# Linear attention into a gated feed-forward layer: weight pieces and block sums in one transfer each, and a new table of ranks

## The chip, the core and the metric

One core of one Trainium2 chip runs the whole kernel. The metric is device time in microseconds (us), the median of several executions. Trace times count from the start of the span, the first instruction of the program.

## What is computed

```python
def phi(x):
    proj = einsum('bhsd,df->bhsf', x, w_phi)
    proj = proj - max(abs(proj), axis=-1, keepdims=True)
    return concatenate([exp(proj), exp(-proj)], axis=-1)
q_p, k_p = phi(q), phi(k)
kv = einsum('bhsf,bhsd->bhfd', k_p, v); z = sum(k_p, axis=2)
num = einsum('bhsf,bhfd->bhsd', q_p, kv)
den = einsum('bhsf,bhf->bhs', q_p, z)[..., None] + 1e-06
x = (num / den) as 4608 tokens x 512            # 8 batches x 576, 8 heads x 64
g = x @ w_gate
out = (silu(g) * (x @ w_val)) @ w_out           # 512 -> 1536 -> 512
```

The three weight matrices are float64, q, k, v and w_phi float32.

## The kernel before

**Attention** works on pairs of heads, 32 pairs in all (8 batches of 4). For a pair it loads k, v and q, projects them on TensorE, takes the largest magnitude on VectorE, the exponentials on ScalarE, and ends with a division and a transposition that write x in two parts, xh (rounded) and xl (the rest). The first eight pairs make the first three chunks of 384 tokens.

**The feed-forward layer** multiplies every number as a rounded part plus a rest, with three matmuls per product (high x high, high x low, low x high), and turns the float64 weights into such parts with a chain on VectorE and ScalarE (weight_piece, lines 382 to 441: lines 403 to 419 are the VectorE steps). The twelve tiles f of the hidden width are converted one after the other while the first three chunks pass, and stored in DRAM: w1_dram for the first layer, w2_dram and w2_whole for the second. The gate of a chunk is lines 896 to 901.

**From chunk 4 on** two chunks at a time are done with seven block products instead of eight, in both layers. For the first layer the operands are seven "units" of weights per f. load_unit (line 1070) loads a pair of units into a slot of the buffers w1 (the trace says w) or of the space a2 (the trace says a); line 1081 is that load, 512 KB for two units. For the second layer the weights are needed as seven "pieces" of 128 x 1536: three are quarters of w_out as it is (BLOCKS 0, 2 and 3), four are sums of such quarters. sums_of_units (line 1234) makes the sums: for each q of six it loads the four quarters of two f into a stage of the buffer spare (line 1238), GpSimd forms the differences (line 1241), line 1246 stores them to w2_sums. piece_of_weights (line 1252) loads one piece (line 1257 for a sum, line 1261 for a quarter), then three copies on ScalarE (line 1267) and three subtractions on VectorE (line 1268) split it. Pieces 0 to 2 are made as soon as the sums are stored, long before the second layer's products (line 1396) begin; pieces 3 to 6 later.

**The order of work** comes from a planner that runs when the program is built. Every instruction, or small group, is a Step with an engine, a cost, the steps it follows and a rank. Plan.run plays the steps through with these costs, takes on each engine the ready step of the lowest rank, and among equal ranks the one added first, and writes the instructions in that order; on the chip each engine then works through its list in order, SyncE's DMA issues among them. Attention pair i has rank i, the feed-forward's short steps FIRST = -1, loads of units and everything of pieces NEXT = -0.5, its matmuls 1000 and up. A DMA is a step of SyncE that takes 0.6 or 0.34 us of it, and the wire for its bytes over BYTES. A load of units must also follow the product that lies 10 us before its use in planned time (ahead(AHEAD[2])):

```python
held[g] = k, first_, add("SP", n * P * 4 * P * 4, lambda: nc.sync.dma_start(...),
    [stored_, *after, ahead(AHEAD[2])], NEXT)
```

The table MOVED gives single steps another rank, by the number of the step in the order of adding. Its keys reach to about 1480 of 5291 steps. Numbers 0 to 455 or so are the attention of the first eight pairs, those up to 1370 the conversion of weights and the first three chunks, the rest up to 1480 belong to pair 8.

Of the kernel before, what the change touches and what calls it, by code (L numbers as in the profile page):

```python
# [59 lines left out]


MOVED = {
# [9 lines left out]


class Step:
# [8 lines left out]
class Plan:  # L83
# [1 line left out]


    LAG = {"PE": 220, "ACT": 90, "DVE": 90, "POOL": 200, "SP": 2000}
    BYTES = 340.0
    BEGIN = {"PE": 1000.0}

    def __init__(self, banks, extra, first):
# [26 lines left out]
    def run(self):  # L118
# [11 lines left out]
        def start(e):  # L130
            nonlocal n, wire, other
            held = []
            got, saved = None, False
            while ready[e]:
                key, s = heapq.heappop(ready[e])
                if s.take is not None and (saved or len(s.take) > sum(len(x) for x in self.lists(s))):
                    held.append((key, s))
                    saved = True
                    continue
                got = s  # L140
                break
            for h in held:
                heapq.heappush(ready[e], h)
            if got is None:
                if e == "PE" and self.fill is not None and pending():
                    cost, fn = self.fill
                    fn()
                    busy[e] = True
                    n += 1
                    heapq.heappush(events, (now + cost, n, "free", e))  # L150
                return
            s = got
            for t in s.take or ():
                self.bank[t] = next(x for x in self.lists(s) if x).pop(0)
            s.fn()
            busy[e] = True
            cost = s.cost
            if e == "PE":
                cost += TURNED if s.rank >= 1000 and other else 0
                other = s.rank < 1000  # L160
            if e == "SP":
                wire = max(wire, now) + s.cost / self.BYTES
                freed, done = now + (600.0 if s.cost < 1e5 else 340.0), wire + s.lag
            else:
                freed, done = now + cost, now + cost + s.lag
            n += 1
            heapq.heappush(events, (freed, n, "free", e))

            for t in s.then:
                n += 1  # L170
                heapq.heappush(events, (freed if t.eng == e and e in ("ACT", "DVE", "PE", "POOL") else done, n, "dep", t))
            if s.give is not None:
                n += 1
                heapq.heappush(events, (done, n, "give", s.give))
# [26 lines left out]

LANDING = {"x": 3000.0, "h": 3000.0, "w": 2500.0, "f": 0.0}
FILL = 200
STRIPS = 350
MERGED = 200
TURNED = 0
KEXP = (1, 0)
BIASED = (0,)  # L210
QEXP = 0
SWITCH = 125
POOLED = 950
INPUT = 1.36
SLOW = 2.0
NEXT_KEYS = 0


# [14 lines left out]


def pe(n):
    return max(58, 7 + 0.441 * n)


def pe32(n):
# [4 lines left out]
def favor_attention_moe(ctx: ExitStack, tc: tile.TileContext, qT, kT, v, w_phi, wg, wv, wo, out):  # L244
# [213 lines left out]
    def keys_of(i, rank):  # L458
# [10 lines left out]
        if i == EARLY_PAIRS + 1:  # L469
            def clear():  # L470
                nc.gpsimd.memset(vf[1]()[:, :, :, D:], 1.0)
                for h in range(2):
# [2 lines left out]
            last["vf", i - 2] = last["kin", i - 2] = last["qin", i - 2] = add("POOL", 1000, clear, weights_done, rank)  # L475
        before = lambda name: [last.get((name, i - 2)), last.get((name + "'", i - 2))]

        k_in = [add("SP", INPUT * P * 4 * P * 4, lambda: nc.sync.dma_start(get(kin[one])[:, :4 * P], kT[b, pr, :, :4 * P]),
                    before("kin"), rank)]
        k_in += [add("SP", P * P, lambda r=slice(h * D, (h + 1) * D), c=4 * P + h * D: nc.sync.dma_start(  # L480
            get(kin[one])[r, c:c + D], kT[b, pr, r, 4 * P:]), before("kin"), rank + 0.1) for h in range(2)]
        n = 4 * P * P
        vm = v[b, pr, :n].rearrange("(p m d) -> p m d", p=P, d=D)
        vr = v[b, pr, n:].rearrange("(p h d) -> p h d", p=D, h=2)
        v_in = [add("SP", INPUT * P * 2 * P, lambda: nc.sync.dma_start(
            get(vf[one])[:, 0:4, :, :D].rearrange("p t h d -> p (t h) d"), vm), before("vf"), rank + 0.2)]
        v_in += [add("SP", P * P, lambda h=h: nc.sync.dma_start(get(vf[one])[h * D:(h + 1) * D, 4, h, :D], vr[:, h]),
                     before("vf"), rank + 0.2) for h in range(2)]


# [95 lines left out]
    def attention(i, rank):  # L586
# [16 lines left out]
        use = lambda name: [last.get((name, i - 2)), last.get((name + "'", i - 2))]  # L603
        before = lambda name: [last.get((name, i - 2)), last.get((name + "'", i - 2))]
        if early:
            q_in = [add("SP", INPUT * P * 4 * P * 4, lambda: nc.sync.dma_start(get(qin[one])[:, :4 * P], qT[b, pr, :, :4 * P]),
                        before("qin"), rank)]
            q_in += [add("SP", P * P, lambda r=slice(h * D, (h + 1) * D), c=4 * P + h * D: nc.sync.dma_start(
                get(qin[one])[r, c:c + D], qT[b, pr, r, 4 * P:]), before("qin"), rank + 0.1) for h in range(2)]
        else:  # L610
            q_in = [add("SP", INPUT * P * S * 4, lambda: nc.sync.dma_start(get(qin[one])[:, :S], qT[b, pr]), before("qin"), rank)]
        merged = late and i + 1 < NB * NPAIR
        if merged:
            keys_of(i + 1, rank + NEXT_KEYS)
# [196 lines left out]
        if any(held):  # L811
            start, width = next((c[2], sum(x[3] for x, y_ in zip(cuts, held) if y_)) for c, x_ in zip(cuts, held) if x_)
            token = b * S + start - PAIRS * CH
            x_stored[b, pr] = add("SP", P * width * 4, lambda start=start, width=width, token=token: nc.sync.dma_start(
                x_dram[pr, :, token:token + width], num[:, start:start + width]), copied, rt)
            last["num", i].append(x_stored[b, pr])
        last["end"] = [*copied, *last["num", i]]
        plan.early = 0
# [18 lines left out]
    def ahead(us):  # L837

        got = [s for t, s in passed if t <= ffn["t"] - 1e3 * us]
        return got[-1] if got else None  # L840


    def parts_of_weights(f, layer, made=None):
# [8 lines left out]
        after = [w_stored[f, layer], *(users[n - sets] if n >= sets else ()), ahead(AHEAD[layer])]  # L852
        if layer:
            return users[-1], t, [add("SP", P * DM * 4, lambda: nc.sync.dma_start(t.bitcast(F32), w2_dram[f]), after, FIRST)]
        return users[-1], t, [add("SP", P * 16 * P * 4, lambda: nc.sync.dma_start(
            t.rearrange("p u h c -> p u (h c)").bitcast(F32), w1_dram[f, :4].rearrange("u p c -> p u c")), after, FIRST)]

    def first(c, f, low):
# [46 lines left out]

    def keep(c, f, j, made):

        th_free[j] = h_kept[c, f] = add("SP", P * CH * 4, lambda: nc.sync.dma_start(h_dram[c, f], get(th[j])), [made], FIRST)

    def fetch(c, f):  # L910
        j = ffn["th"] % TH_SETS
# [80 lines left out]
    def sums_of_weights(f, rank):  # L992
# [1 line left out]
        gp = nc.gpsimd  # L994
        x = lambda u: full()[:, u]
        s = sums_w
        done = [add("SP", P * 8 * P * 4, lambda: nc.sync.dma_start(
            full().rearrange("p (s u) c -> p s (u c)", s=2), w1_whole[f].rearrange("s p c -> p s c")),
                    [w_stored[f, 4], *full_free], rank)]
        for o, l, r in ((0, 2, 0), (2, 3, 2), (3, 3, 0), (1, 1, 3)):  # L1000
# [226 lines left out]
    NQ = NFT // 2  # L1227
    BLOCKS = (0, 2, None, None, None, 3, None)
    SUM_OF = {2: 1, 3: 2, 4: 0, 6: 3}
    part_of = lambda u, q: w2_whole[2 * q + u // 2, :, u % 2 * 2 * P:(u % 2 + 1) * 2 * P]  # L1230
    sum_stages = [spare[:, 7 * 2 * P * n:7 * 2 * P * (n + 1)].rearrange("p (u c) -> p u c", u=7) for n in range(2)]
    stage_free, sums_made, pieces_read = [[], []], [], []

    def sums_of_units(q):

        gp = nc.gpsimd
        sum_stage, free = sum_stages[q % 2], stage_free[q % 2]
        done = [add("SP", INPUT * P * 2 * P * 4, lambda u=u: nc.sync.dma_start(sum_stage[:, u], part_of(u, q)),
                    [w_stored[2 * q + u // 2, 5], *free, ahead(1)], NEXT) for u in range(4)]
        for o, l, r in ((4, 3, 1), (5, 1, 0), (6, 3, 5), (0, 2, 6)):  # L1240
            done = [add("POOL", POOLED, lambda o=o, l=l, r=r: gp.tensor_tensor(
                out=sum_stage[:, o], in0=sum_stage[:, l], in1=sum_stage[:, r], op=ALU.subtract), done, NEXT)]
# [9 lines left out]
    def piece_of_weights(n, stage, free, hi, lo, home_free):  # L1252

        j = n
        rank = NEXT + (1e-3 * (1 + n) if n > 2 else 0)
        if BLOCKS[j] is None:
            got = [landing(add("SP", P * 1536 * 4, lambda: nc.sync.dma_start(
                stage().rearrange("p (s c) -> p s c", s=NQ // 2),
                w2_sums[SUM_OF[j]].rearrange("s p a c -> p s (a c)")), [*sums_made, *free], rank), "w")]
        else:  # L1260
            got = [landing(add("SP", INPUT * P * 2 * P * 4, lambda q=q: nc.sync.dma_start(
                stage()[:, 2 * P * q:2 * P * (q + 1)], part_of(BLOCKS[j], q)), [w_stored[2 * q + BLOCKS[j] // 2, 5], *free], rank), "w")
                for q in range(NQ)]
        made, read = [], []
        for k in range(3):
            c = slice(2 * DM // 2 * k, 2 * DM // 2 * (k + 1))
# [77 lines left out]
    def second_pair(index, c):  # L1344
# [13 lines left out]
        def load(name, chunk, e):  # L1358
            for q in range(N2):
                at, after = grab()  # L1360
                tile_of[name, q] = at
                made[name, q] = landing(add("SP", P * 2 * CH * 4, lambda at=at, f=4 * q + e: nc.sync.dma_start(
                    at().rearrange("p (f t) -> p f t", f=2), h_dram[chunk, f:f + 3:2].rearrange("f p t -> p f t")),
                    [h_kept[chunk, 4 * q + e], h_kept[chunk, 4 * q + e + 2], *after, ahead(SOON[3] - 3 * len(made))], turn(0)), "h")

# [210 lines left out]
```

## Time and profile before

| | |
|---|---|
| runs of the kernel | 1126.70, 1126.67 and 1132.02 us, median 1126.7 |
| the profiled execution, its own time | 1130.88 us |
| its span, first to last instruction | 1129.0 us |
| granted TensorE clock, mean over the span | 0.998 |
| busy: TensorE, VectorE, ScalarE, GpSimd | 1110.5, 887.7, 628.6, 110.6 us |
| moved by DMA | 269.56 MB, 239 GB/s over the span |

The profile is of one execution. A row names a line of the kernel, an engine (PE is TensorE's matmul, DVE VectorE, ACT ScalarE, POOL GpSimd, SP SyncE; a q behind it means its sequencer), an operation, the tiles it writes and reads, and its times. Idle time is put down to what ended it. The clock is given as a share of 2.4 GHz: 1.00 is that, 0.5 is 1.2 GHz, and a value between is an average over a stretch with both.

### The profile page before, as it was taken

What the parts mean: (1) busy time and instruction counts of PE and PEld (TensorE: products, weight loads), DVE (VectorE), ACT (ScalarE), POOL (GpSimd) and SP (SyncE); (2) the same over time, 40 slices, a digit from 0 to 9 for tenths busy, and PEclk for the clock granted to TensorE, in tenths of its full rate; (3) what the DMA queues carried; (4) which work ended last, traced back from release to release, by engine and by line L of the source; (5) the groups of instructions that cost most, each with busy time, mean ns of one, the idle gap of its engine ahead of it and who ended that gap; (6) DMA issues with size and microseconds to landing.
All of it is one profiled execution on the core that took longest, in us unless ns stands there. A gap on an engine that the chain in (4) does not pass through costs nothing.

```text
span 1129.0 us, 28084 instructions
## 1 busy us (share of the span) xinstructions
PE 1110.5 (98%) x11172; PEld 1058.3 (94%) x11172; DVE 887.7 (79%) x1418; ACT 628.6 (56%) x1373; POOL 110.6 (10%) x192
## 2 busy tenths in 40 slices
PE   8998999999999999999999999999999999999998
PEld 7887999999888998999999999999998999999998
DVE  6989999778878787788888989968556567979663
ACT  6885333356676675676667666744334345444342
POOL 0000000012122112322210010100420000000000
PEclk9999999999999999999999999999999999999999
DMA  5639998657888777889989897779996788652511
GB/s 159 180 103 319 309 331 299 212 179 220 241 255 276 237 225 260 252 291 312 320 244 288 279 321 242 244 241 348 287 319 211 262 273 285 206 168 85 183 42 43
DMA packets 193298, 269.56 MB, mean 239 GB/s; under 512 B 56464, under 2 KB 106640, under 8 KB 193168
## 3 DMA queue, kind: packets, MB, share of 16 engines
q1 hardware_dynamic: 192864, 267.64, 73.4%
q8 instruction: 88, 1.44, 0.5%
q14 instruction: 42, 0.34, 0.1%
q10 hardware_dynamic: 304, 0.13, 0.0%
HBM read 187.50 MB, written 80.22 MB: 237 GB/s over the span
## 4 chain that ended last, share of the span: by engine, by line
PE 90%; DVE 3%; DMA 3%; ACT 2%; issue 1%; SPq 1%; POOL 0%; ACTq 0%; DVEq 0%; POOLq 0%
PE gv L376 17%; PE gv L1148 14%; PE o L1148 14%; PE o L376 10%; PE work L1396 7%; PE work L376 5%; PE work L560 5%; PE gv L1396 5%; PE o L1396 5%; PE work L747 4%; PE work L787 1%; PE work L569 1%; DMA a<-w_dram 1%; DMA w_dram<-a 1%; DMA a<-in_qT_dram 1%
## 5 line engine op out<-in xcount | busy, mean ns | idle before, releaser
L376 PE MATMUL gv<-xh,w 128*128 128x384 f32 x768 | 210.0, 339 | 3.0 <-DVE m L898 3.0
L376 PEld LDWEIGHTS gv<-xh,w 128*128 128x128 f32 x768 | 139.9, 188 | 5.6 <-DVE m L898 3.9
L376 PE MATMUL gv<-xl,w 128*128 128x384 f32 x384 | 128.8, 335 | 0.1
L376 PE MATMUL o<-w_hi,hidden 128*128 128x512 f32 x288 | 103.3, 403 | 0.0
L1148 PE MATMUL gv<-xh,w 128*128 128x384 f32 x336 | 99.2, 339 | 0.0
L1148 PE MATMUL o<-m,w 128*128 128x384 f32 x388 | 81.8, 339 | 0.2 <-ACT snap L1158 0.2
L376 PEld LDWEIGHTS gv<-xl,w 128*128 128x128 f32 x384 | 72.2, 188 | 1.2 <-DVE xl L805 0.4
L1148 PEld LDWEIGHTS o<-m,w 128*128 128x128 f32 x388 | 69.1, 189 | 0.8 <-ACT snap L1158 0.6
L1161 DVE TENSOR_TENSOR snap<-o,snap 128x384 f32<-128x384 f32 x72 | 39.9, 554 | 33.9 <-PE o L1148 28.0
L376 PEld LDWEIGHTS o<-w_hi,hidden 128*128 128x128 f32 x288 | 54.1, 188 | 10.6
L1148 PEld LDWEIGHTS gv<-xh,w 128*128 128x128 f32 x336 | 61.8, 188 | 0.3
L1161 DVE TENSOR_TENSOR snap<-gv,snap 128x384 f32<-128x384 f32 x72 | 39.9, 555 | 26.2 <-PE gv L1148 20.0
L1168 ACT ACTIVATE m<-snap 128x384 f32<-128x384 f32 x47 | 24.7, 526 | 58.0 <-DVE snap L1161 57.9
L376 PE MATMUL o<-w_lo,hidden 128*128 128x512 f32 x144 | 56.9, 395 | 0.0
L1148 PE MATMUL gv<-xl,w 128*128 128x384 f32 x168 | 56.5, 336 | 0.0
L1148 PE MATMUL o<-xh,w 128*128 128x384 f32 x188 | 55.3, 340 | 0.0
L747 PE MATMUL work<-m,m 128*64 128x65 f32 x1696 | 54.4, 221 | 0.0
L1158 ACT COPY snap<-gv 128x384 f32<-128x384 f32 x72 | 34.2, 475 | 35.5 <-PE gv L1148 18.8
L1158 ACT COPY snap<-o 128x384 f32<-128x384 f32 x72 | 34.3, 476 | 35.3 <-PE o L1148 17.8
L518 DVE TENSOR_REDUCE km<-work 128x4 f32<-128x512 f32 (+1 forms) x84 | 46.3, 552 | 8.3 <-PE work L376 7.6
L747 PEld LDWEIGHTS work<-m,m 128*64 128x64 f32 x1696 | 51.9, 138 | 0.5 <-issue 0.5
L1001 POOL TENSOR_TENSOR m<-m 128x256 f32<-128x256 f32 x48 | 38.5, 802 | 91.0 <-DMA m<-w_whole 53.7
(446 smaller groups left out, 3073.3 us busy)
## 6 DMA issues: line engine op xcount, KB each, us to landing
w<-w_dram SPq DMA_DIRECT2D x113, 512.0 KB, 5.0
h_dram<-m SPq DMA_DIRECT2D x90, 192.0 KB, 4.3
w_dram<-w SPq DMA_DIRECT2D x12, 1024.0 KB, 5.8
w_dram<-a SPq DMA_DIRECT2D x24, 512.0 KB, 4.3
w<-w_dram SPq DMA_DIRECT2D x12, 1024.0 KB, 6.6
w<-w_dram SPq DMA_DIRECT2D x38, 256.0 KB, 4.3
w_lo<-w_dram SPq DMA_DIRECT2D x36, 256.0 KB, 3.8
spare<-h_dram SPq DMA_DIRECT2D x19, 384.0 KB, 4.0
```

Of the source, the lines that this page charges most:

```text
L376: nc.tensor.matmul(o, l, r, start=a, stop=z)
L518: kmax = add("DVE", dve(n * NF), lambda m=m, view=view: vec.tensor_reduce(out=m, in_=view(), axis=AX.X, op=ALU.max, apply_absolute_value=T ...
L560: nc.tensor.matmul(o[c, n:n + D2], kp[h][:, t, k, c], get(vf[one])[:, t, h], start=t + k == 0, stop=False)
L569: nc.tensor.matmul(work[plan.bank[names[h]]][c, n:n + D2], kp[2][r, 0, k, c], get(vf[one])[r, 4, h], start=False, stop=k == 1)
L747: nc.tensor.matmul(o[c * D:(c + 1) * D, t * D2:(t + 1) * D2], (qe, qx)[k][j][:, h, n:n + D], kvs[j][:, (2 * h + k) * D2:(2 * h + k + 1) * D2],
L787: nc.tensor.transpose(o[:, m * P:(m + 1) * P], x, ident)
L1001: done = [add("POOL", POOLED, lambda o=o, l=l, r=r: gp.tensor_tensor(out=x(o), in0=x(l), in1=x(r), op=ALU.subtract), done, rank)]
L1148: nc.tensor.matmul(o[:, :CH], l, r, start=begin and i == 0, stop=i == len(terms) - 1, skip_group_check=True)
L1158: return add("ACT", act(CH), lambda: act_.copy(snap[n], bank[:, :CH]), [after, *snap_free[n]], FIRST)
L1161: return add("DVE", dve(CH), lambda: vec.tensor_tensor(out=snap[n], in0=bank[:, :CH], in1=snap[n], op=ALU.add), after, FIRST)
L1168: t0 = add("ACT", act(CH), lambda: act_.activation(get(t_), get(x), AF.Tanh, scale=0.5), [*after, th_free[j]], FIRST)
L1396: nc.tensor.matmul(cut(o, t - ts[0], W), l, r, start=begin and q == 0 and m == 0 and t == ts[0], stop=q == NQ - 1 and m == 2, skip_group_c ...
```

## The change

In sums_of_units four loads of 128 KB become one of 512 KB, for each q. In piece_of_weights six loads of 128 KB become one of 768 KB, for pieces 0, 1 and 5, and pieces 0 to 2, loads and conversion, go from rank NEXT to NEXT + 0.0005. The planner's numbers change: bytes per ns, the issue time of a large transfer, the factors on loads of inputs and of weights, the cost of a matmul, and the landing of stores. MOVED gets 116 entries in place of 83; in both tables most are of the first eight pairs, some of the weights' conversion (numbers 467 to 711), and a few of pair 8.

```diff
 MOVED = {
-    0: 0.08, 11: 0.93, 13: 0, 61: 2.83, 66: 0.22, 67: -0.29, 75: 0.34, 81: 1.44, 104: 0.09, 109: 0.56, 112: 2.13,
...
+    3: 0.63, 5: -2.74, 11: 0.98, 20: -3.33, 34: -3.64, 57: 1.05, 58: 1.04, 62: 7.86, 63: -3.3, 70: 1, 72: 16.52,
...
-    BYTES = 340.0
+    BYTES = 400.0
...
-                freed, done = now + (600.0 if s.cost < 1e5 else 340.0), wire + s.lag
+                freed, done = now + (600.0 if s.cost < 1e5 else 450.0), wire + s.lag
...
-LANDING = {"x": 3000.0, "h": 3000.0, "w": 2500.0, "f": 0.0}
+LANDING = {"x": 3000.0, "h": 3000.0, "w": 2500.0, "store": -700.0}
-MERGED = 200
+MERGED = 400
-INPUT = 1.36
-SLOW = 2.0
+INPUT = 1.3
+SLOW = 1.5
+TAIL = 4.5
...
-    return max(58, 7 + 0.441 * n)
+    return max(58, 4 + 0.441 * n)
...
-        k_in = [add("SP", INPUT * P * 4 * P * 4, lambda: nc.sync.dma_start(get(kin[one])[:, :4 * P], kT[b, pr, :, :4 * P]),
+        k_in = [add("SP", P * 4 * P * 4, lambda: nc.sync.dma_start(get(kin[one])[:, :4 * P], kT[b, pr, :, :4 * P]),
...
-        k_in += [add("SP", P * P, lambda r=slice(h * D, (h + 1) * D), c=4 * P + h * D: nc.sync.dma_start(
+        k_in += [add("SP", TAIL * P * P, lambda r=slice(h * D, (h + 1) * D), c=4 * P + h * D: nc.sync.dma_start(
...
-        v_in = [add("SP", INPUT * P * 2 * P, lambda: nc.sync.dma_start(
+        v_in = [add("SP", 1.6 * P * 4 * P * 4, lambda: nc.sync.dma_start(
...
-        done = [add("SP", INPUT * P * 2 * P * 4, lambda u=u: nc.sync.dma_start(sum_stage[:, u], part_of(u, q)),
-                    [w_stored[2 * q + u // 2, 5], *free, ahead(1)], NEXT) for u in range(4)]
+        done = [add("SP", P * 2 * DM * 4, lambda: nc.sync.dma_start(
+            sum_stage[:, :4].rearrange("p (e v) c -> p e (v c)", e=2), w2_whole[2 * q:2 * q + 2].rearrange("e p c -> p e c")),
+            [w_stored[2 * q, 5], w_stored[2 * q + 1, 5], *free, ahead(1)], NEXT)]
...
-        rank = NEXT + (1e-3 * (1 + n) if n > 2 else 0)
+        rank = NEXT + 1e-3 * (1 + n if n > 2 else 0.5)
...
-            got = [landing(add("SP", INPUT * P * 2 * P * 4, lambda q=q: nc.sync.dma_start(
-                stage()[:, 2 * P * q:2 * P * (q + 1)], part_of(BLOCKS[j], q)), [w_stored[2 * q + BLOCKS[j] // 2, 5], *free], rank), "w")
-                for q in range(NQ)]
+            e, v = divmod(BLOCKS[j], 2)
+            got = [landing(add("SP", 1.1 * P * 1536 * 4, lambda: nc.sync.dma_start(
+                stage().rearrange("p (q c) -> p q c", q=NQ),
+                w2_whole.rearrange("(q e) p c -> e p q c", e=2)[e][:, :, 2 * P * v:2 * P * (v + 1)]),
+                [*(w_stored[2 * q + e, 5] for q in range(NQ)), *free], rank), "w")]
```

The stores of x and of the hidden chunks (lines 814 and 908) are given the "store" landing, and the loads of q, of first-layer weights and of hidden chunks get factors of the same kind; these are edits of planner costs alone.

## Rows read from the trace of the kernel before

**Rows 1.** The page, part 1: busy time of each engine, share of the span, instructions.

```profile
PE 1110.5 (98%) x11172; PEld 1058.3 (94%) x11172; DVE 887.7 (79%) x1418; ACT 628.6 (56%) x1373; POOL 110.6 (10%) x192
```

**Rows 2.** Waits of TensorE, whole span: us in total, times, longest us.

```profile
PE gv L376 <- DVE m L898: 3.0, 3, 1.7
PE gv L1148 <- DMA a<-w_dram: 2.7, 1, 2.7
PE work L569 <- issue: 2.1, 2, 2.0
```

**Rows 3.** Timeline of TensorE, 848 to 859 us: start, us, instruction, [idle before <-releaser].

```profile
848.22 1.21 PE L1148 MATMUL o<-m,a 128*128 128x384 f32 x6
849.27 1.23 PE L1148 MATMUL o<-m,w 128*128 128x384 f32 x6
853.19 0.41 PE L1148 MATMUL gv<-xh,a 128*128 128x384 f32 x1 [2.69 <-DMA a<-w_dram]
...
854.32 2.04 PE L1148 MATMUL o<-m,w 128*128 128x384 f32 x6
...
857.97 0.34 PE L1148 MATMUL gv<-xh,w 128*128 128x384 f32 x1
```

**Rows 4.** Stretch 853 to 856 us: PE, PEld, DVE, ACT, POOL busy, PEclk, DMA share, GB/s.

```profile
853.00:856.00 3.00, 2.81 (x12) 2.84 (x13) 0.00 (x0) 1.43 (x3) 0.00 (x0) 0.73 0.63 237
```

**Rows 5.** Chain of waits, 840 to 860 us: start, us, what.

```profile
835.52 4.85 DMA h_dram<-m
...
840.38 0.35 SPq L1261
...
844.45 8.60 DMA a<-w_dram
```

**Rows 6.** Timeline of SyncE's DMA issues, 835 to 846 us: start, us, issues.

```profile
836.17 3.03 SPq L1261 DMA_DIRECT2D spare<-w_whole  x5
...
839.88 4.00 SPq L1261 DMA_DIRECT2D spare<-w_whole  x7
843.92 0.43 SPq L1257 DMA_DIRECT2D spare<-w_sums  x1
844.45 0.43 SPq L1081 DMA_DIRECT2D a<-w_dram  x1
```

**Rows 7.** The page, part 6: issues of one kind, KB each, median us to landing.

```profile
w<-w_dram SPq DMA_DIRECT2D x113, 512.0 KB, 5.0
```

**Rows 8.** Line 1238, loads for the block sums: issue ns min/median/max, first and last start.

```profile
L1238 SPq DMA_DIRECT2D spare<-w_whole x24: 319/424/757, 788.3 to 825.9; - x24
```

**Rows 9.** Line 1268 on VectorE, then the chain of waits at 920 to 930 us.

```profile
L1268 DVE TENSOR_TENSOR hidden<-spare,w_lo x3: 681/685/687, 858.7 to 861.8; 128x512 fp32r<-128x512 f32 x3
...
926.10 3.91 PE work L1396 x33
```

**Rows 10.** Timeline of TensorE, 94 to 107 us: waits for VectorE.

```profile
94.88 0.33 PE L787 MATMUL o<-ident,m 128*128 128x128 f32 x1 [1.19 <-DVE m L771]
...
100.06 0.44 PE L376 MATMUL gv<-xh,w 128*128 128x384 f32 x1 [0.69 <-DVE m L898]
...
106.17 0.44 PE L376 MATMUL gv<-xh,w 128*128 128x384 f32 x1 [1.66 <-DVE m L898]
```

**Rows 11.** VectorE, 80 to 108 us, by line: busy us, mean ns, idle before.

```profile
L416 DVE TENSOR_TENSOR a<-a 128x1024 f32<-128x1024 f32 x2 | 2.5, 1226 | 0.1
L413 DVE SCALAR_TENSOR_TENSOR a<-a,a 128x1024 f32<-128x1024 uint32 x2 | 2.4, 1222 | 0.0
L419 DVE TENSOR_TENSOR w<-a,w 128x1024 fp32r<-128x1024 f32 x2 | 2.4, 1217 | 0.0
...
L408 DVE SCALAR_TENSOR_TENSOR a<-a,a 128x1024 uint32<-128x1024 uint32 x1 | 1.2, 1219 | 0.0
```

**Rows 12.** Stretch 84.67 to 112.90 us, columns as in rows 4.

```profile
84.67:112.90 28.23, 24.56 (x318) 22.19 (x315) 27.24 (x47) 16.69 (x36) 0.00 (x0) 1.00 0.91 319
```

More of the change, by code (lines that the diff above doesn't have):

```diff
@@ L484, in keys_of @@
         vr = v[b, pr, n:].rearrange("(p h d) -> p h d", p=D, h=2)
-        v_in = [add("SP", INPUT * P * 2 * P, lambda: nc.sync.dma_start(
+        v_in = [add("SP", 1.6 * P * 4 * P * 4, lambda: nc.sync.dma_start(
             get(vf[one])[:, 0:4, :, :D].rearrange("p t h d -> p (t h) d"), vm), before("vf"), rank + 0.2)]
-        v_in += [add("SP", P * P, lambda h=h: nc.sync.dma_start(get(vf[one])[h * D:(h + 1) * D, 4, h, :D], vr[:, h]),
+        v_in += [add("SP", TAIL * P * P, lambda h=h: nc.sync.dma_start(get(vf[one])[h * D:(h + 1) * D, 4, h, :D], vr[:, h]),
                      before("vf"), rank + 0.2) for h in range(2)]
@@ L605, in attention @@
         if early:
-            q_in = [add("SP", INPUT * P * 4 * P * 4, lambda: nc.sync.dma_start(get(qin[one])[:, :4 * P], qT[b, pr, :, :4 * P]),
+            q_in = [add("SP", P * 4 * P * 4, lambda: nc.sync.dma_start(get(qin[one])[:, :4 * P], qT[b, pr, :, :4 * P]),
                         before("qin"), rank)]
-            q_in += [add("SP", P * P, lambda r=slice(h * D, (h + 1) * D), c=4 * P + h * D: nc.sync.dma_start(
+            q_in += [add("SP", TAIL * P * P, lambda r=slice(h * D, (h + 1) * D), c=4 * P + h * D: nc.sync.dma_start(
                 get(qin[one])[r, c:c + D], qT[b, pr, r, 4 * P:]), before("qin"), rank + 0.1) for h in range(2)]
         else:
-            q_in = [add("SP", INPUT * P * S * 4, lambda: nc.sync.dma_start(get(qin[one])[:, :S], qT[b, pr]), before("qin"), rank)]
+            q_in = [add("SP", P * S * 4, lambda: nc.sync.dma_start(get(qin[one])[:, :S], qT[b, pr]), before("qin"), rank)]
         merged = late and i + 1 < NB * NPAIR
@@ L813, in attention @@
             token = b * S + start - PAIRS * CH
-            x_stored[b, pr] = add("SP", P * width * 4, lambda start=start, width=width, token=token: nc.sync.dma_start(
-                x_dram[pr, :, token:token + width], num[:, start:start + width]), copied, rt)
+            x_stored[b, pr] = landing(add("SP", P * width * 4, lambda start=start, width=width, token=token: nc.sync.dma_start(
+                x_dram[pr, :, token:token + width], num[:, start:start + width]), copied, rt), "store")
             last["num", i].append(x_stored[b, pr])
@@ L854, in parts_of_weights @@
             return users[-1], t, [add("SP", P * DM * 4, lambda: nc.sync.dma_start(t.bitcast(F32), w2_dram[f]), after, FIRST)]
-        return users[-1], t, [add("SP", P * 16 * P * 4, lambda: nc.sync.dma_start(
+        return users[-1], t, [add("SP", 1.35 * P * 16 * P * 4, lambda: nc.sync.dma_start(
             t.rearrange("p u h c -> p u (h c)").bitcast(F32), w1_dram[f, :4].rearrange("u p c -> p u c")), after, FIRST)]
@@ L906, in keep @@
     def keep(c, f, j, made):
-        th_free[j] = h_kept[c, f] = add("SP", P * CH * 4, lambda: nc.sync.dma_start(h_dram[c, f], get(th[j])), [made], FIRST)
+        th_free[j] = h_kept[c, f] = landing(add("SP", P * CH * 4, lambda: nc.sync.dma_start(h_dram[c, f], get(th[j])), [made], FIRST), "store")
     def fetch(c, f):
@@ L996, in sums_of_weights @@
         s = sums_w
-        done = [add("SP", P * 8 * P * 4, lambda: nc.sync.dma_start(
+        done = [add("SP", 1.3 * P * 8 * P * 4, lambda: nc.sync.dma_start(
             full().rearrange("p (s u) c -> p s (u c)", s=2), w1_whole[f].rearrange("s p c -> p s c")),
@@ L1229, in favor_attention_moe @@
     SUM_OF = {2: 1, 3: 2, 4: 0, 6: 3}
-    part_of = lambda u, q: w2_whole[2 * q + u // 2, :, u % 2 * 2 * P:(u % 2 + 1) * 2 * P]
     sum_stages = [spare[:, 7 * 2 * P * n:7 * 2 * P * (n + 1)].rearrange("p (u c) -> p u c", u=7) for n in range(2)]
@@ L1361, in load @@
                 tile_of[name, q] = at
-                made[name, q] = landing(add("SP", P * 2 * CH * 4, lambda at=at, f=4 * q + e: nc.sync.dma_start(
+                made[name, q] = landing(add("SP", 1.07 * P * 2 * CH * 4, lambda at=at, f=4 * q + e: nc.sync.dma_start(
                     at().rearrange("p (f t) -> p f t", f=2), h_dram[chunk, f:f + 3:2].rearrange("f p t -> p f t")),
```

19 rows, old and new, of the table MOVED are left out of this document.

## The prediction

> **What bounds the kernel now.** I began with the page: TensorE is busy 1110.5 of the span's 1129.0 us [rows 1]. That share hides how little there is to win: the idle time is 1129.0 - 1110.5 = 18.5 us in all, and every useful matmul stays as it is. So the question is which part of 18.5 us the change can reach, and the second view is the list of what TensorE waited for [rows 2]. Its first three lines are three waits for VectorE's gate of the first chunk (line 898, 3.0 us), one wait for a DMA into a buffer of space "a", which is the load of units of first-layer weights by line 1081 (2.7 us), and two waits named "issue" (2.1 us), which no operand causes. The rest is idle time at the two ends and single short waits.
>
> The DMA wait is the one to follow. The timeline of TensorE shows it between 850.50 and 853.19 us, and shows that it costs more than its length [rows 3]. A group of six matmuls takes 849.27 - 848.22 = 1.05 us. From 849.27 to 857.97 there are four such groups (those that start at 849.27, 853.19, 854.32 and 856.16), which at that pace need 4.20 us and took 8.70. The loss is 4.5 us, not 2.7. The rest is the clock: after the idle stretch the granted clock is 0.73 on average from 853 to 856 [rows 4], a mixture of the levels 1.2 and 2.4 GHz, and the group at 854.32 lasts 2.04 us where the one at 848.22 lasts 1.21.
>
> The chain of waits tells why the unit came late [rows 5]. Its load was issued at 844.45 and landed 8.60 us later, where the median load of that size takes 5.0 [rows 7]. Before its issue the chain runs through SyncE's own queue, on line 1261, which loads the pieces of second-layer weights, and there it goes back to a store that landed at 840.37: SyncE did not merely spend time on issuing, it also stood until an older transfer was done. The timeline of SyncE shows the whole block [rows 6]: twelve piece loads of 128 KB (5 from 836.17 for 3.03 us, 7 from 839.88 for 4.00 us), the load of a sum, then the unit's load. By the code, pieces and units had the same rank, and the pieces were added earlier.
>
> **The change, part by part.** *Pieces 0 and 1 in one transfer each, ranked behind units.* Twelve issues become two. At the 0.43 us that the issue at 843.92 took, they need 0.86 us in place of 3.03 + 4.00 = 7.03. The unit load may go out when the products are within 10 us of its use (AHEAD[2]); its use would come at 849.27 + 1.05 = 850.32, so it is due at about 840.3. With the landing time it had in the bad case, 8.60 us, it must be issued by 850.32 - 8.60 = 841.7. Two issues, or none of lower rank, ahead of it at 840.3 leave it in time. I take the whole loss as gone: **-4.5 us**. The bounds are 0 (it is late again) and -4.5, as no other work is on TensorE's path there. What is late next: nothing close by that the list of waits names, the next DMA wait of TensorE doesn't exist in it.
>
> *Their later conversion.* The copies and subtractions of pieces 0 to 2 take a rank just behind NEXT, so they may go after other work of VectorE and ScalarE. The last one starts at 861.8 now and lasts 0.69 us; the first product that reads a piece starts at 926.10 [rows 9]. That is 926.10 - 862.5 = 63.6 us of cover, so zero. If the cover were gone, each conversion would cost at most its 0.69 us. A piece also lands in one block of 768 KB instead of six of 128 KB; since each conversion waited for all six already, no reader waits longer for that reason.
>
> *Inputs of the block sums.* Twenty-four loads of 128 KB become six of 512 KB. At the median of 0.424 us an issue [rows 8], 24 take 10.2 us and six 2.5, so SyncE gets 7.6 us back between 788 and 826. GpSimd waits for these loads and TensorE doesn't wait for GpSimd. Zero, unless it delays the pieces, which have 63.6 us. Piece 5 goes from six loads to one, and the one DMA wait that TensorE has lies elsewhere: zero as well.
>
> *Costs of the planner.* BYTES, INPUT, TAIL, pe(), MERGED, the issue time and the landing of stores are numbers by which the planner orders the work; none is an instruction. They can change the order on all five engines, SyncE's and GpSimd's queues included, and no view shows the new order. The same holds for the *new table of ranks*, which moves 116 steps where the old one moved 83: attention of the first eight pairs, the conversion of the first weights on VectorE, and a few loads and steps of pair 8. I bound both together from the stretch where order counts. Between 84.67 and 112.90 us VectorE is busy 27.24 of 28.23 us while TensorE stands [rows 12], and three of TensorE's waits for VectorE there are 1.19, 0.69 and 1.66 us, 3.54 in all [rows 10]. A better order wins at most these, as VectorE has under 1 us of idle time to give in that stretch: -3.5. A worse order puts weight conversions in front of what TensorE needs. The long ones (lines 408, 413, 416, 419) last 1.219, 1.222, 1.226 and 1.217 us [rows 11], together 4.88 us for one first-layer weight piece; two pieces and one fall of the clock (the 4.5 us above less 2.69 of idle and the 0.18 between 850.32 and 850.50, so about 1.6) make +11.4. Between -3.5 and +11.4 I take 0: the nearest row is that of VectorE's load, which is near full whatever the order, and the old table had left no idle time of TensorE in that stretch beyond waits of 1 to 2 us.
>
> **Sum.** The profiled execution took 1130.88 us (1129.0 of span and 1.9 around it). 1130.9 - 4.5 + 0 = 1126.4 on its own footing. The median of the runs, 1126.7, is 4.2 us under the profiled one, and one of the three runs shown is 1132.0. Carried over to the median: 1126.7 - 4.5 = **1122.2 us**, 0.4% less. A measurement of this kernel can tell about 0.5%, 5.6 us, from no change; so the likeliest single result lies just inside "the same".
>
> **Rivals.** *The order of the early steps gains too.* The three waits of 3.54 us go along with the DMA wait: 1122.2 - 3.5 = 1118.7. For it: they are waits for single instructions of VectorE, so a swap of neighbours can move them. Against it: VectorE's 27.24 of 28.23 us.
>
> *The stall stays, or the median never had it.* Merging takes away issues and not bytes. If the two big pieces go out just ahead of the unit load, it has 1.5 MB in front of it as before, its landing stays at 8.60 us, and any issue after 841.7 makes TensorE stand. Also, 4.2 us between the profiled run and the median is close to the 4.5 us of this loss, so the two quick runs may be executions in which it was small. Either gives 1126.7. For it: the slack from 840.3 to 841.7 is 1.4 us only. Against it: the rank lets a unit that is due go first. The Trainium skill speaks for this rival (DMA: Bandwidth & Descriptors, section "Queues, rings and completion order"): each DMA engine takes the descriptors of one ring in order, so a transfer waits for all that was issued before it on that ring. By that rule alone, with the pieces first, the sum would be 1126.7; the trace's 8.60 us against 5.0 agrees with it.
>
> *Slower.* The place is VectorE before 113 us, the mechanism that conversions of two first-layer weight pieces go ahead of the gates of line 898 and the steps of line 771. Price, as above, 11.4 us; with the 4.5 us won later 1122.2 + 11.4 = 1133.6. It decides from 4.5 us of conversions on, that is a little less than one piece (4.88); one piece without the clock's fall gives 1122.2 + 4.9 = 1127.1. For it: VectorE is full there, and the new table again moves steps of the conversion of the first weights. Against it: later products also need those conversions, so an order that runs them early isn't lost time altogether.
>
> **How the numbers follow.** Forecast 0.40, both gains 0.30, no gain 0.18, slower 0.12. Faster by over 0.5% (under 1121.1) is the second case and 0.07 of the first, for small gains of order: 0.37. Slower by over 0.5% (over 1132.3) is two thirds of the last: 0.08. The same is the rest, 0.55. The range goes from 1116.5, the second case with about 2 us of the small waits elsewhere (the "issue" waits of 2.1 among them), to 1129.0, which takes in no gain, with 2.3 us for one new wait of the length of the old one, and one displaced piece. It leaves out about 2 in 10, most of it the slower end.
>
> **What would show it.** Right: no wait of TensorE for a load of line 1081, a granted clock of 1.00 after 850 us, three piece loads of 768 KB in place of 18, and the unit load in that stretch issued 8 us or more before its first product. The term of zero is right if the early waits for VectorE sum to about 3.5 us again. Wrong: a wait for a unit load or a landing over 8 us close to its use; TensorE idle in 84 to 113 us much over or under 3.7 us; or new waits of TensorE of over a us in the middle, where the list has only the "issue" wait. If a profile without the stall goes with a median that didn't move, the median never had it.

## The result and the profile after

The change makes the kernel slower: 1136.02 us, the median of 15 runs (1130.53 to 1140.91), against 1128.23 for 15 runs of the kernel before in the same job (1124.51 to 1132.02). The ratio is 1.0064 [1.0049, 1.0080]. I had said 1122.2, with 0.08 for slower and 1129.0 as the upper end. The profiled execution took 1134.96 us against 1130.88, its span is 1133.2 against 1129.0, and its mean granted clock 0.997 against 0.998. The lines of the kernel after stand 4 below those of before up to the products of chunk pairs (line 1148 is now 1152), and 5 or 6 below further on.

The page, part 1, and TensorE's list of waits (us in total, times, longest), after:

```profile
PE 1115.3 (98%) x11189; PEld 1061.6 (94%) x11189; DVE 892.8 (79%) x1418; ACT 629.6 (56%) x1373; POOL 109.0 (10%) x192
```

```profile
PE gv L380 <- DVE m L902: 3.4, 3, 1.4
PE gv L380 <- DMA m<-in_kT_dram: 2.7, 2, 1.8
PE work L791 <- DVE m L775: 2.3, 2, 1.9
...
PE o L1152 <- DMA w<-w_dram: 1.0, 2, 0.7
PE gv L1152 <- DMA w<-w_dram: 0.9, 1, 0.9
```

The wait that I followed is gone: the list has no 2.7 us for a load into space "a" [rows 2]. New are the second and the third line, neither of them near the second-layer weights, and three short waits for units, 1.9 us in all. TensorE's busy time grew by 4.8 us [rows 1] although its useful matmuls are the same. In part that is the clock, which fell to half twice, near 12 and near 305 us, and before once: slower matmuls count as busy for longer.

TensorE around 850 us, and two stretches (PE, PEld, DVE, ACT, POOL busy, PEclk, DMA share, GB/s), after:

```profile
849.91 0.51 PE L1152 MATMUL gv<-xh,w 128*128 128x384 f32 x2
850.26 0.34 PE L1152 MATMUL gv<-xl,w 128*128 128x384 f32 x1
```

```profile
840.00:870.00 30.00, 30.00 (x173) 29.79 (x172) 19.31 (x36) 11.56 (x25) 0.00 (x0) 1.00 0.62 219
853.00:856.00 3.00, 3.00 (x20) 3.00 (x19) 2.09 (x4) 0.89 (x2) 0.00 (x0) 1.00 0.99 345
```

TensorE runs through, at a granted clock of 1.00, where before it was 2.81 of 3.00 us busy at 0.73 [rows 3, 4]. SyncE's issues, after:

```profile
828.86 3.29 SPq L1266 DMA_DIRECT2D spare<-w_whole  x2
832.19 0.54 SPq L1261 DMA_DIRECT2D spare<-w_sums  x1
```

```profile
836.06 0.44 SPq L1085 DMA_DIRECT2D w<-w_dram  x1
836.60 0.41 SPq L1085 DMA_DIRECT2D a<-w_dram  x1
...
839.71 0.42 SPq L1085 DMA_DIRECT2D w<-w_dram  x1
```

Pieces 0 and 1 are two transfers and leave at 829 us, ahead of the units that leave from 836 us on; the block of twelve loads [rows 6] isn't there. To see where the time went I gave every form of matmul its normal duration and counted for each stretch how much longer it took, before and then after: 0 to 30 us 9.2 and 12.5; 226 to 340 us 3.8 and 8.4; 340 to 480 us 7.1 and 4.8; 790 to 840 us -0.2 and 1.4; 840 to 870 us 4.4 and 0.0; 940 to 1000 us 0.6 and 1.7. All stretches together make the 4.2 us of the spans. So the 4.4 us around 850 were won as worked out, and more was lost at three other places. Why 340 to 480 us got shorter was not looked into.

**The first 16 us.** The first k load and the first projection before, then SyncE's wait, its first issues and TensorE's waits for inputs after:

```profile
1.21 0.41 SPq L478 DMA_DIRECT2D m<-in_kT_dram  x1
```

```profile
4.67 1.16 PE L376 MATMUL gv<-wst,m 64*128 64x128 f32 x16
```

```profile
SPq L491 <- POOL m L365: 2.0, 1, 2.0
```

```profile
2.21 0.57 SPq L491 DMA_DIRECT2D m<-in_v_dram  x1
2.84 0.57 SPq L482 DMA_DIRECT2D m<-in_kT_dram  x1
```

```profile
5.90 1.16 PE L380 MATMUL gv<-wst,m 64*128 64x128 f32 x16 [0.84 <-DMA m<-in_kT_dram]
...
12.31 2.08 PE L380 MATMUL gv<-wst,m 64*128 64x128 f32 x16 [1.84 <-DMA m<-in_kT_dram]
```

The new table gives step 5 (the last rows of v of the first pair, line 491) the value -2.74, so its load leads SyncE's queue. Its buffer is first cleared by GpSimd (line 365), so SyncE stands until 2.21 us with every other load behind it. Before, the first k load went out at 1.21 us and the first projection began at 4.67; now it is 2.84 and 5.90. At 12.31 the second pair's projection follows a wait of 1.84 us and lasts 2.08 us where the first lasted 1.16.

**300 to 312 us.** GpSimd; then VectorE; then TensorE; then stretches in the columns above, after:

```profile
298.27 0.73 POOL L1005 TENSOR_TENSOR m<-m 128x256 f32<-128x256 f32 x1 [21.04 <-DMA m<-w_whole]
299.06 0.21 POOL L712 COPY qu<-qm 64x36 f32<-64x36 f32 x1
299.35 1.95 POOL L1005 TENSOR_TENSOR m<-m 128x256 f32<-128x256 f32 x2
301.37 0.20 POOL L714 COPY qu<-qm 32x36 f32<-32x36 f32 x1
301.65 0.75 POOL L1005 TENSOR_TENSOR m<-m 128x256 f32<-128x256 f32 x1
302.46 0.20 POOL L709 COPY qu<-qu 32x36 f32<-32x36 f32 x1
302.73 0.21 POOL L710 COPY qu<-qu 64x36 f32<-64x36 f32 x1
```

```profile
302.97 1.38 DVE L718 STREAM_TRANSPOSE m<-qu 128x1152 f32<-128x1152 f32 x1 [1.05 <-POOL qu L710]
304.27 0.71 DVE L775 TENSOR_TENSOR m<-work,rc 128x256 f32<-128x256 f32 x2
```

```profile
305.04 0.66 PE L791 MATMUL work<-ident,m 128*128 128x128 f32 x4 [1.92 <-DVE m L775]
```

```profile
304.00:308.00 4.00, 2.96 (x12) 2.33 (x12) 3.85 (x8) 1.91 (x5) 0.00 (x0) 0.73 0.73 189
308.00:312.00 4.00, 4.00 (x28) 3.17 (x27) 2.47 (x4) 2.18 (x5) 0.00 (x0) 0.84 0.90 268
```

Four sums of first-layer weights (line 1005) waited on GpSimd for a load and then ran between the four copies that an attention pair needs (lines 712, 714, 709, 710). VectorE's transposition of the copied values waits for the last copy, the division (line 775) stands behind it on VectorE, and TensorE waits for the division: 1.92 us, then a clock below 1.00.

**785 to 795 us.** Chain of waits (start, us, what), after:

```profile
786.36 8.44 DMA w<-w_dram
```

A load of units took 8.44 us to land. Less than 3 us before it, from 783.56 on, the first two of the new 512-KB loads for the block sums had been issued, and after them two other loads of units; which of the four held it isn't shown. The landing of 8.60 us [rows 5] has a successor here, though TensorE's waits for it are short (0.89 and 0.28 us).

### The profile page after: what moved, and what is told of

Same layout as the page of the kernel before. It is cut to its first block, busy times and chain, and to the rows that moved or that the text cites. A ratio compares the mean times of both kernels' runs of the same rounds, so it can differ in the third digit from the quotient of the medians.

```text
span 1133.2 us, 28098 instructions
## 1 busy us (share of the span) xinstructions
PE 1115.3 (98%) x11189; PEld 1061.6 (94%) x11189; DVE 892.8 (79%) x1418; ACT 629.6 (56%) x1373; POOL 109.0 (10%) x192
## 4 chain that ended last, share of the span: by engine, by line
PE 88%; DMA 5%; DVE 2%; ACT 1%; SPq 1%; issue 1%; POOL 1%; DVEq 0%; POOLq 0%; ACTq 0%
PE gv L380 16%; PE o L1152 14%; PE gv L1152 14%; PE o L380 9%; PE work L1402 6%; PE work L380 5%; PE work L564 5%; PE gv L1402 5%; PE o L1402 4%; PE work L751 4%; DMA w<-w_dram 1%; PE work L791 1%; PE work L573 1%; DMA h_dram<-m 1%; DMA m<-w_whole 1%
```

## The experiments

Unless the text says otherwise, a kernel computes everything and differs by the edit shown. Times are medians, with the median of the kernel before in the same job and the interval of the ratio.

**The parts by themselves.** First the merged transfers and the rank of pieces 0 to 2 on the kernel before (the last hunks of the change); then the kernel after without these; then the kernel after with the old MOVED; then the kernel before with the new planner numbers alone (all hunks but those and MOVED).

```diff
merge_only: before
+ one load per q in sums_of_units, one per quarter in piece_of_weights
+ rank = NEXT + 1e-3 * (1 + n if n > 2 else 0.5)
no_merge:   after, the same two parts undone
old_table:  after, MOVED of before
costs_only: before, BYTES, INPUT, SLOW, TAIL, pe(), MERGED, LANDING, issue time, factors of after
```

> The kernel before with the merged transfers and the lower rank of pieces 0 to 2, under the old planner costs and the old table: nothing differs up to 784 us. Theory P (the merges take the 2.7 us wait at 850 us and the clock's fall behind it away, and the loss of the whole change comes from costs and table): ratio to before 0.996, 4 to 5 us faster, no wait of TensorE for a unit load after 835 us. Rival Q (big transfers in front of unit loads delay them, and the loss comes from there): 1.000 or above, waits for unit loads of 1 us and more between 784 and 830 us. Rival R (the median of before never had that wait): 1.000 though the profile shows no wait at 850 us.

> The whole change without the merges and without the new rank of pieces: new costs and new table alone. Theory P: the loss of costs and table stands alone, 1.008 to 1.012, with the late start (first projections 1.2 us later) and the waits at 240 to 310 us as in the changed kernel. Rival Q: below the changed kernel, 1.003 or less.

> The whole change with the old table of ranks: merges and new costs. If the new table makes the loss (its v-tail load at the head of SyncE's queue among it): 0.998 or below. If the new costs make it: 1.005 or above, as in the changed kernel.

> The kernel before with the new planner costs alone, old table, no merges. If the costs make the loss: 1.005 to 1.012. If the table makes it: 0.998 to 1.003. Against old_table it gives the merges once more: 4 to 5 us more than old_table by theory P, about the same by R.

| kernel | us | before | ratio |
|---|---|---|---|
| merge_only | 1126.20 | 1127.38 | 0.9982 [0.9970, 0.9995] |
| no_merge | 1140.93 | 1127.38 | 1.0112 [1.0090, 1.0134] |
| old_table | 1145.75 | 1127.38 | 1.0167 [1.0130, 1.0204] |
| costs_only | 1149.51 | 1127.38 | 1.0208 [1.0159, 1.0257] |

The transfers win 0.2% alone and 0.4% to 0.5% in the other two pairs (1.0112 to 1.0064, 1.0208 to 1.0167), which is less than the luck of an order that is measured further on. The planner's numbers cost 2%, and the new table gives back half of that. TensorE's waits, merge_only, then no_merge, then costs_only:

```profile
PE gv L376 <- DVE m L898: 3.0, 3, 1.7
```

```profile
PE gv L1152 <- DMA w<-w_dram: 6.5, 2, 4.9
```

```profile
PE gv L1149 <- DMA w<-w_dram: 7.4, 4, 3.4
```

With the merge on the old numbers the early waits are those of before [rows 2], they head the list, and the one wait for units in it is of 0.4 us. With the new numbers and no merge the wait for units is back and larger: 4.9 us of no_merge's 6.5 lie between 840 and 870 us.

**Rank or merge?** One line of the change, on the kernel before:

```diff
-        rank = NEXT + (1e-3 * (1 + n) if n > 2 else 0)
+        rank = NEXT + 1e-3 * (1 + n if n > 2 else 0.5)
```

> The kernel before with the lower rank of pieces 0 to 2 and nothing else: the unit load goes ahead of five of the twelve piece loads and of the load of the sum. If the place in SyncE's queue was what delayed the unit load: no wait of TensorE at 850 us, or under 1 us, and 0.998. If the bytes in front of it on the rings were (ring order): the load still lands 8 us or more after its issue and TensorE waits 1.5 us or more, 1.000.

1126.62 us against 1129.26, ratio 0.9977 [0.9956, 0.9998]: as much as with the merge. SyncE's issues and the stretch in the columns above, rank_only:

```profile
841.62 0.38 SPq L1081 DMA_DIRECT2D a<-w_dram  x1
842.04 2.37 SPq L1261 DMA_DIRECT2D spare<-w_whole  x5
```

```profile
840.00:870.00 30.00, 30.00 (x174) 30.00 (x173) 21.16 (x38) 14.25 (x30) 0.00 (x0) 1.00 0.71 246
```

The unit's load now leaves at 841.62 instead of 844.45, ahead of five piece loads and the sum's. That is the 841.7 that the prediction worked out, and TensorE doesn't wait. In the kernel before, the rank alone does it. The load also landed after 4.11 us in place of 8.60, with five piece loads and the sum's load less in front of it. The merge gets there by another way. In merge_only both large pieces and the sum's load still leave ahead of the unit (835.01 to 837.20 us); its load leaves at 840.53, takes 8.86 us and lands 1.9 us before its use. With merged loads of the old rank the planner writes the program of merge_only, instruction for instruction, so there the rank adds nothing.

**Is it a wrong number, or any other order?** A cost that is 1 ns other is no better or worse a guess, yet it leads the planner to another order. So the kernel before got pe() with 6 in place of 7, and, apart from that, BYTES 400 alone:

```diff
nudge:      -    return max(58, 7 + 0.441 * n)
            +    return max(58, 6 + 0.441 * n)
bytes_only: -    BYTES = 340.0
            +    BYTES = 400.0
```

> The kernel before with one planner number moved by a hair: the constant of a matmul's cost 6 ns in place of 7, old table. Nothing about DMA changes. Theory F (the old table fits one exact order; any change of the costs reshuffles the order and loses that fit): 1.008 to 1.02, about as costs_only. Theory B (the new costs are wrong for this chip, the DMA ones above all): 0.998 to 1.003.

> The kernel before with BYTES 400 in place of 340 alone, old table. Theory B: 1.012 or above, with waits of TensorE for unit loads as in costs_only. Theory F: like nudge, within 0.006 of it, whichever way.

nudge took 1137.46 us against 1128.31, ratio 1.0077 [1.0050, 1.0104], bytes_only 1153.70, ratio 1.0227 [1.0197, 1.0258]. One nanosecond costs 0.8%. TensorE's waits in nudge:

```profile
PE gv L1148 <- DMA w<-w_dram: 3.5, 1, 3.5
PE gv L1148 <- ACT w_lo L1267: 3.1, 1, 3.1
PE gv L376 <- DVE m L898: 3.0, 3, 1.7
```

No new wait is early, where the table has most of its entries; they are at products of chunk pairs. BYTES alone costs as much as all the new numbers together.

**Without a table**, so that no fit to one order is in the way: MOVED = {} with the old numbers, with BYTES 400, with pe() 6 or 8, with all the new numbers, and with all of them but BYTES, each without the merges.

```diff
+MOVED = {}
no_table_old:    old numbers         no_table_bytes: BYTES = 400.0
no_table_nudge:  6 + 0.441 * n       no_table_nudge2: 8 + 0.441 * n
no_table_new:    new numbers         no_table_rest:  new numbers, BYTES = 340.0
```

> The kernel before without any table of ranks, old costs. Theory F: the old table was worth the whole difference, 1.012 to 1.025, as costs_only or worse. Theory B: the table matters less, 1.000 to 1.010.

> New costs, no table, no merges. Theory F: the same as no_table_old within 0.005, because without a table neither set of costs is fitted to. Theory B: over 0.010 above no_table_old.

> The kernel before without a table and with BYTES 400 alone. If BYTES is the wrong number among the new costs: 1.025 or above, as the full set of new costs without a table (1.0287). If it is another of them: about 1.014, as the old costs without a table.

> New costs except BYTES, which stays 340; no table, no merges. If the other new costs carry the loss beside BYTES: 1.022 or above (1.0287 less what BYTES alone adds, 1.0195 - 1.014). If BYTES carries it together with them: 1.014 to 1.018.

> Old costs, no table, the constant of a matmul's cost 6 ns in place of 7: a new order without a reason to be better or worse. If without a table the order is not fitted and such luck is small: 1.014 within 0.003. If luck of the order is as large as the effect of the new costs: off by 0.007 or more, either way, and the 0.0147 between old and new costs without a table says little.

> The same with 8 ns: a second draw. Small luck: 1.014 within 0.003; large luck: off by 0.007 or more.

| kernel | us | before | ratio |
|---|---|---|---|
| no_table_old | 1144.49 | 1128.31 | 1.0140 [1.0109, 1.0172] |
| no_table_nudge | 1134.03 | 1129.27 | 1.0038 [1.0018, 1.0058] |
| no_table_nudge2 | 1142.39 | 1129.27 | 1.0136 [1.0089, 1.0183] |
| no_table_rest | 1136.21 | 1129.27 | 1.0060 [1.0036, 1.0083] |
| no_table_bytes | 1149.14 | 1129.26 | 1.0195 [1.0164, 1.0227] |
| no_table_new | 1160.93 | 1128.31 | 1.0287 [1.0247, 1.0327] |

A nanosecond more or less moves the time of an order without a table by up to 1.0140 - 1.0038 = 1.0%. That is the luck of an order, and a single pair of kernels says little below it. But the groups part: the four with BYTES 340 lie between 1.0038 and 1.0140, the two with 400 above them all. The kernels whose table didn't fit their numbers stand the same way (nudge with 340 at 1.0077; old_table, costs_only and bytes_only with 400 at 1.0167 to 1.0227). The other new numbers aren't shown to do harm: no_table_rest lies within the luck. It and no_table_bytes came out outside both of the values expected for them, so these four and two draws are few.

The runs also show what the old table is worth: 1.4% on the numbers of the kernel before (no_table_old), and nothing once a number is moved. With pe() 6 the kernel takes 1.0077 with it and 1.0038 without, with BYTES 400 1.0227 and 1.0195.

**The places in the kernel after.** To leave the order as it is but for one place, these kernels let the planner write down its order for the kernel after, move the steps named, and emit that list; emitted without a move, it is the program of the kernel after, instruction for instruction. late_v_tail moves step 5 behind the other loads of the first pair, late_sums the four sums of 300 us (steps 2881 to 2884) behind the pair's copies, late_both does both.

```diff
late_v_tail: + tail = log.pop(at_.index(5))
             + log.insert([x[0] for x in log].index(4) + 1, tail)
late_sums:   + subs = [log[at_.index(n)] for n in range(2881, 2885)]
             + log = [x for x in log if x not in subs]
             + k = [x[0] for x in log].index(1637) + 1
             + log[k:k] = subs
```

> The changed kernel in its own exact order, with one DMA moved: the small load of v that stands first in SyncE's queue goes behind the other loads of the first pair. If that load holds up the start, because its buffer is first cleared by GpSimd: the first k load is issued before 1 us in place of 2.84, the first projection starts at about 4.7 us in place of 5.90, and 1 to 2 us come off the 1.0064: 1.005. Rival: the start moves and the gain is lost by 113 us, where VectorE is full: 1.0064.

> The changed kernel in its own exact order, with four GpSimd instructions moved: one block's sums of first-layer weights go behind the four copies of an attention pair instead of between them. If those sums, which wait for a load of 7.5 us, make TensorE's wait of 1.9 us at 303 us and the fall of the clock after it: that wait is gone, the clock stays at 1.00 there, and 2 to 4 us come off: 1.003 to 1.005. Rival: the copies are late for another reason, the wait stays: 1.0064.

> The changed kernel in its own exact order with both moves, the v load and the four GpSimd sums. If the two losses are separate: 1.0064 - 0.0022 - 0.0017 = 1.0025, still slower than before, with the first projection near 5.0 us and no wait at 303 us. If one hides the other: 1.004.

| kernel | us | before | ratio |
|---|---|---|---|
| late_v_tail | 1133.72 | 1129.26 | 1.0042 [1.0021, 1.0063] |
| late_sums | 1132.97 | 1129.26 | 1.0047 [1.0029, 1.0065] |
| late_both | 1130.65 | 1129.27 | 1.0006 [0.9993, 1.0019] |

In late_both SyncE's first issue, GpSimd at 298 us, and two stretches in the columns above are:

```profile
0.74 0.40 SPq L485 DMA_DIRECT2D m<-in_kT_dram  x1
```

```profile
297.51 0.21 POOL L712 COPY qu<-qu 32x36 f32<-32x36 f32 x1 [0.28 <-DVE qu L708]
297.78 0.21 POOL L713 COPY qu<-qu 64x36 f32<-64x36 f32 x1
298.07 3.18 POOL L1009 TENSOR_TENSOR m<-m 128x256 f32<-128x256 f32 x4
```

```profile
300.00:304.00 4.00, 4.00 (x22) 3.32 (x21) 3.06 (x5) 1.98 (x5) 1.17 (x2) 1.00 0.32 94
304.00:308.00 4.00, 4.00 (x31) 3.12 (x30) 3.88 (x8) 3.52 (x7) 0.00 (x0) 1.00 0.94 254
```

One load and four short sums, out of 5,000 steps, carry 1.0064 - 1.0006 = 0.58% of the loss; between 300 and 308 us TensorE is busy all the time at full clock. Alone they gave 0.22% and 0.17%, which the intervals don't tell from nothing; only both together are clear of them.

The profiles divide it less evenly. TensorE's wait for a load of q and a stretch in late_both, then the wait near 302 us in late_v_tail, whose sums still run between the copies:

```profile
PE work L383 <- DMA m<-in_qT_dram: 1.9, 1, 1.9
```

```profile
26.00:30.00 4.00, 2.25 (x17) 2.06 (x18) 2.10 (x5) 3.94 (x15) 0.00 (x0) 0.72 0.76 212
```

```profile
302.08 0.66 PE L794 MATMUL work<-ident,m 128*128 128x128 f32 x4 [0.62 <-DVE m L778]
```

In late_both the earlier start is lost again before 30 us, to a wait that ends at 27.7 us and the fall of the clock with it; in that execution the count by stretches puts the whole gain over the kernel after between 226 and 340 us. In late_v_tail the sums cost 0.62 us and no fall, so their place alone doesn't make the 1.92 us. What separates late_both from merge_only's 0.9982, some 2.7 us, is no more than that new wait and its fall would explain; that they do was not tried, nor the load of 8.44 us near 790 us.

Faster than both kernels are merge_only and rank_only, by 0.2% on the kernel before, at the edge of what a measurement can tell.

## Why the prediction was wrong

**The sign came from the term "costs of the planner", valued at 0.** That step of the prediction took 0 from VectorE's load before 113 us and bounded it by -3.5 and +11.4 there. no_merge, which has exactly what the term covers, new numbers and new table, measured 1.0112, some 14 us where 0 was taken, and over the upper bound as well. Numbers alone, with the old table, cost 1.0208, some 22 us (costs_only); the new table takes that back only in part. The bound was made from the wrong stretch: a planner's costs reorder everything, and what the kernel after lost lies at 0 to 30, 226 to 340 and 790 to 840 us. In the stretch that I looked at, VectorE is a little less busy now:

```profile
84.67:112.90 28.23, 25.48 (x406) 23.07 (x405) 26.16 (x49) 18.88 (x47) 0.00 (x0) 1.00 0.56 182
```

That is 26.16 us against 27.24 [rows 12], and TensorE's three waits for the gate take 3.4 us against 3.0 [rows 2, 10]. So the slower rival had the right sign and the wrong place: conversions of weights stand before the gates in both kernels, and the gates wait 0.4 us longer, not 11.4. (The range's 2.3 us for a new wait of the length of the old one should have been 2.69; that changes nothing here.)

**Why the costs lose.** Two things can be said, at different strength. Better supported: the old table fits one order, as its 1.4% is gone after 1 ns on a cost or with BYTES 400; the 0.8% that the 1 ns loses is one draw and within the luck of 1.0%. By a tendency over eleven kernels that lack the transfers or a fitting table: plans made with BYTES 400 run 1.1% to 2.9% longer than the kernel before, those made with 340 0.4% to 1.4%. The 1.1% is no_merge, the one with the table made for its numbers; among the other ten the two groups don't overlap. The kernel after, with 400, that table and the transfers, is at 0.64%. The likeliest reason is that the planner then thinks loads land earlier than they do, and lets them go later or in larger heaps. For it, the waits for loads of units in costs_only (7.4 us) and no_merge (6.5 us); on the page of the kernel after the fastest of forty slices moved 363 GB/s. Against taking that as settled, the transfers do reach that rate in places (398 GB/s in late_both between 785 and 800 us), and bytes_only's largest waits are for VectorE's gate of line 898 (4.9 us); it is argued, not shown.

**The transfers: right in mechanism, too large in size.** Around 850 us each sign that was named came: no wait for units, a clock of 1.00 at 853 us, three large piece loads, units that leave ahead of need. Of the signs against it three came elsewhere: waits for units (1.9 us in all), a landing of 8.44 us close to its use, and a new wait of 1.92 us in the middle. Rank or merge suffices alone for the stall, by rank_only and merge_only. But the term of -4.5 us gave 0.18% in merge_only and 0.23% in rank_only, some 2.0 and 2.6 us. In the plan of the kernel after it gave 0.48%, some 5 us, where the wait that it took away was 4.9 us (no_merge).

The fault is the step that carried the profiled run's loss over to the median. In rank_only's job 14 of the 29 runs of before had a mean granted clock of 1.000, and their median, 1126.4 us, is that of rank_only, 1126.6; the other 15, at 0.997 to 0.998, had 1130.7. Of the ten runs of rank_only nine were at 1.000. So it seems that about half the executions of before lost some 4.3 us, and half nothing that shows; the rival "the median never had it" was half right. Whether the runs at 1.000 had the idle 2.69 us without the fall, or not at all, stays open, as no such execution of before has a profile here; the 4.3 us are more than the 1.6 that the prediction worked out for the fall, which speaks for less idle time too.

"The stall stays" had the landing right and the issue wrong: in merge_only the unit's load still took 8.86 us behind the large pieces, but left at 840.53, before the 841.7 that this rival named. The rule that spoke for it (the Trainium skill, DMA: Bandwidth & Descriptors, section "Queues, rings and completion order": each DMA engine takes the descriptors of one ring in order) agrees with these 8.86 us and the 4.11 of rank_only, with less in front, where the median is 5.0 [rows 7].

**The terms of zero for later conversions and for sum inputs** held for the conversions in the kernel after: their loads leave at 829 to 832 us, far ahead of the products. They belong to that order, though: in nudge a wait of TensorE of 3.1 us is put down to such a conversion (line 1267). The sum loads may not have come quite free, as they stand ahead of units near 784 us.

**The order of early steps gains too** came in its own stretch and was outweighed. From 84.67 to 112.90 us TensorE is idle for 2.75 us in place of 3.67, but the first 30 us lost 3.3 us. One entry of the new table may make much of that: late_v_tail's median gives 0.22% or 2.5 us, within the intervals.

## What to carry to other kernels

A number that only steers a planner is no small edit: bound it by the difference between whole orders, which a few harmless nudges of a cost measure, and not by the stretch that looks fullest. Take a hand-fitted table as part of that exact order; keep costs and table, and add a transfer's merge or rank on top of them. Before a stall is counted as a gain, ask how many executions have it: the profiled one here stood 4.2 us over the median, almost exactly the loss that I meant to win.

## What the runs showed of the chip beyond that

The same order of instructions runs with and without a fall of the clock: in rank_only's job the kernel before showed a mean of 1.000 in 14 runs and less in 15. Where a profile shows the fall, the clock dropped after TensorE stood for about 2 us (1.84, 1.92 and 2.69 us) and stayed at half for 3.4 us, as the 0.73 and 0.84 of two stretches of 4 us at 304 to 312 us make it; the 2.69 us cost 4.5 in all. Standing as long doesn't always bring it. In costs_only TensorE's wait and the two stretches around it are:

```profile
858.74 0.41 PE L1149 MATMUL gv<-xh,w 128*128 128x384 f32 x1 [2.58 <-DMA w<-w_dram]
```

```profile
855.00:858.70 3.70, 1.16 (x7) 0.84 (x5) 3.51 (x7) 1.73 (x4) 0.00 (x0) 1.00 1.06 403
858.70:864.00 5.30, 5.26 (x30) 5.29 (x31) 2.75 (x6) 2.48 (x5) 0.00 (x0) 1.00 1.02 375
```

The clock stays at 1.00 after 2.58 us of standing.

A load at the head of SyncE's queue that waits for GpSimd's clearing of a buffer held all others for 1.5 us (first issue at 2.21 us, in late_both at 0.74). And 512-KB loads behind larger heaps landed after 8.44 us in the kernel after and 8.60 in the one before, against a median of 5.0 [rows 7]; the load that took 8.60 took 4.11 in rank_only, with less in front of it.
